# VectorE and ScalarE in source order, and 0.6 of a weight unit per round, in an attention-and-FFN kernel

## The chip, the cores and the metric

The kernel runs on one core of one Trainium2 chip. The metric is the device time of one execution in microseconds (us). Three runs of the kernel before gave 956.33 us as the median (955.23 to 957.48).

## What is computed

Three stages follow each other; the reference, cut to what matters here:

```python
q_s, k_s = q * scale, k * scale                      # 4 batches, 8 heads, 576 tokens, 64 wide
h = einsum('bhsd,md->bhsm', x, omega) - sum(x*x)/2   # phi, 128 features
q_p, k_p = exp(h - max(h)) / sqrt(m)
num = q_p @ (k_p.T @ v); den = q_p @ sum(k_p)
x = num / (den + 1e-6)                               # 2304 tokens, 512 wide
xn = x / rms(x) * rms_g
x = (silu(xn @ w_gate) * (xn @ w_val)) @ w_out       # FFN, 1536 wide
logits = x @ w_gate2                                 # routes 288 tokens to each of 8 experts
out[mask_e] = relu(x[mask_e] @ w1[e]) @ w2[e]
```

The FFN weights arrive as 64-bit floats and the chip turns them into 32-bit ones. Matrix products that need the precision are done as three products of a high and a low part.

## The kernel before

**Rounds.** The first stage is a loop over 93 rounds (`run_tick`, L748). Each round starts one of 88 items: a K item (a projection of keys, features, and k-times-v sums) or a Q item (half of a tile of queries). An item goes through lags 0 to 5, one lag a round, so that up to six items are alive in a round: lag 0 projects (TensorE, L377 to L379, into `pp`), takes the maximum (VectorE, `mx`, L386) and exponentials (ScalarE, `ft`, L389); lag 1 multiplies K features with v (L423) or transposes Q features (L465), which ScalarE copies (`qp`, L482); lag 2 of a Q item is L469 with `dn` and `x` on VectorE (L489 to L491); lag 3 squares on ScalarE (L497); lag 4 scales `xn` on VectorE (L502); lag 5 transposes `xn` (L474), and ScalarE and VectorE write its high and low parts `xh` (L512) and `xl` (L513). At the end of a round the input of the next item is split: a K item's `kh` on ScalarE and `kl` on GpSimd (L352, L353), a Q item's `qh` on VectorE and `ql` on GpSimd (L372, L373). The next round's projection needs both.

**FFN steps.** From round 25 on a round also runs an FFN half-step ("step" below): 12 matmuls (L605 to L607) of one 512-token block j against one 128-wide slice f of the gate (v = 0) or value (v = 1) weights, into one of the two `gv` buffers in PSUM. After a gate step ScalarE takes tanh (L616) and VectorE multiplies (`th`, L617); after a value step VectorE multiplies (`hp` L625 for block 0, `th` L629 for the others). There are 120 steps. Blocks share two buffers, so before a third block is begun the loop at L756 runs the remaining steps of the oldest block at once. Steps that don't fit into the rounds follow behind them.

**Units.** A unit converts 512 columns of weights: a load of 512 KB from HBM (L529, three buffers `ws`), lag 0 a magnitude on ScalarE (L533, into one of three buffers `dw`), lag 1 three shift-and-or operations on VectorE (L537 to L539, called words below), lag 2 a ScalarE cast (L561) and a GpSimd subtraction (L562) into the weight tile `wc`. Behind lag 1 of a unit the load three units ahead is issued. 24 units (two for each f) make the gate and value weights. 12 more make the output weights; these also use TensorE (L576, L580) and hold a `gv` buffer from lag 2 to lag 3. A step runs only if both units of its f are converted; a step with outstanding logits (L643) also needs the output unit of that slice.

**What sets the order.** TensorE works in the order of the source (`manual_schedule`, L778). The other engines' orders come from a scheduler that ranks instructions by priority when the program is built; the attention work has a priority 200 places ahead of its source position. On the chip each engine takes its instructions in the order built, and waits at the first that isn't ready.

**The pace.** `conv_pe` (L731) adds a pace to an account and starts a unit for each whole one: 0.5 a round up to round 24, 1.0 from round 25 while gate and value units are left, then 0.5. From round 25, while such units are left, L771 to L776 do a second helping in each round: one more unit and one more step. So six rounds (25 to 30) run two units and two steps each.

Of the kernel before, what the change touches and what calls it, by code (L numbers as in the profile page):

```python
# [31 lines left out]
KF = FF // 128  # L32
# [11 lines left out]
EARLY = 6  # L44
LOADS = 9
SKIP = 2
SUB = 1
PACE = (0.5, 1.0, 0.5)
FFN_AT = 25
AHEAD_A = 200  # L50
HB = 6
# [239 lines left out]
def kernel(ctx, tc, qT, kT, v1, om, wgv, rms, wo, wg2, w1, w2, cfd, trd, cid, out, dbg=None):  # L291
# [307 lines left out]
    def ffn_pe(j, f, v):  # L599
        n = WIDTH[j]  # L600
        pg = psG.tile([128, BLK], F32, name="gv")
        w = wsl[f].rearrange("p l (v k m) -> p l v k m", k=KD, v=2)
        xh, xl = xblk[j]
        for k in range(KD):
            nc.tensor.matmul(pg[:, :n], w[:, 0, v, k], xh[:, k, :n], start=(k == 0), stop=False)  # L605
            nc.tensor.matmul(pg[:, :n], w[:, 0, v, k], xl[:, k, :n], start=False, stop=False)  # L606
            nc.tensor.matmul(pg[:, :n], w[:, 1, v, k], xh[:, k, :n], start=False, stop=(k == KD - 1))  # L607
        return pg[:, :n]

    def ffn_el(j, f, v, pg):  # L610
        n = WIDTH[j]
        nh = n // HB2
        if v == 0:
            fst["th"] = fp.tile([128, BLK], F32, name="th")
            th = fst["th"][:, :n]
            nc.scalar.activation(th, pg, AF.Tanh, scale=0.5)  # L616
            nc.vector.scalar_tensor_tensor(th, th, 1.0, pg, op0=OP.add, op1=OP.mult)  # L617
            return
        th = fst["th"][:, :n]
        hp = fp.tile([128, BLK // HB2, 2, HB2], F32R, name="hp")  # L620
        hf = hp.bitcast(F32)
        dst = h_dr[nh * j:nh * j + nh] if nh > 1 else h_dr[NT // HB2 - 1:]
        dst = dst[:, :, f].rearrange("b p x -> p b x")
        if j == 0:
            nc.vector.scalar_tensor_tensor(hf[:, :, 0], pg.rearrange("p (b t) -> p b t", b=nh), 0.5,  # L625
                                           th.rearrange("p (b t) -> p b t", b=nh), op0=OP.mult, op1=OP.mult)
            nc.sync.dma_start(dst[:, :, :HB2], hf[:, :, 0])
            return
        nc.vector.scalar_tensor_tensor(th, pg, 0.5, th, op0=OP.mult, op1=OP.mult)  # L629
        h = th.rearrange("p (b t) -> p b t", b=nh)  # L630
        nc.scalar.copy(hp[:, :nh, 0], h)  # L631
        nc.gpsimd.tensor_sub(hp[:, :nh, 1], h, hp[:, :nh, 0])  # L632
        nc.sync.dma_start(dst, hf[:, :nh].rearrange("p b l t -> p b (l t)"))
        fq.append((j, f, hp))

    def ffn_lg(j, f, hp):
        n = WIDTH[j]
        nh = n // HB2
        if f == 0:
            st["lg", j] = (psL if j else psB).tile([2 * E, BLK], F32, name="lg" if j else "late", bufs=1)  # L640
        wv = wog[:, f].rearrange("p a e -> p (a e)")
        lg = st["lg", j][:, :n].rearrange("p (b t) -> p b t", b=nh)
        nc.tensor.matmul(lg, wv, hp[:, :nh, 0], start=(f == 0), stop=False)  # L643
        nc.tensor.matmul(lg, wv, hp[:, :nh, 1], start=False, stop=(f == KF - 1))
        if f == KF - 1:
            ls = fp.tile([2 * E, BLK], F32, name="th")
            nc.scalar.copy(ls[:, :n], st.pop(("lg", j))[:, :n])
            lgs.append((j, ls))

    def ffn_rank():  # L650
        for j, ls in lgs:
            n, c = WIDTH[j] // 128, j * BLK // 128
            pl = psL.tile([128, BLK // 128, 2 * E], F32, name="lg")
            for i in range(n):
                nc.tensor.transpose(pl[:, i, :], ls[:, i * 128:(i + 1) * 128], ident[:2 * E, :2 * E])
            lt = fp.tile([128, BLK // 128, E], F32, name="lt")
            nc.scalar.copy(lt[:, :n], pl[:, :n, E:])
            nc.vector.tensor_add(L[:, c:c + n, :], pl[:, :n, :E], lt[:, :n])
            rks.extend(range(c, c + n, 2))
        lgs.clear()  # L660

    def ffn_rank_el():
        for c0 in rks:
            ranks(nc, fp, cf[:, C_T:C_N].rearrange("p (a b) -> p a b", b=E), L, R, c0, 2)
        rks.clear()

    def ffn_step_pe():
        if not ready or ready[0][1:] not in gvs or (fq and fq[0][1] not in wogs):
            return False
        j, f, v = ready.pop(0)  # L670
        pg = ffn_pe(j, f, v)
        if (f, v) == (KF - 1, 1):
            del xblk[j]
        ffn_rank()
        if v and fq:
            ffn_lg(*fq.pop(0))
        fst["el"] = (j, f, v, pg)
        return True

    def ffn_step_el():  # L680
        if "el" in fst:
            j, f, v, pg = fst.pop("el")
            ffn_el(j, f, v, pg)
            ffn_rank_el()
            return j, f, v
        return None


    items = []
# [3 lines left out]
    useq = [WgvUnit(f, g) for f in range(KF) for g in range(2)] + [WoUnit(f) for f in range(KF)]  # L693
# [30 lines left out]
    def warm(n):  # L724
        for _ in range(n):
            nc.tensor.matmul(sink, idle[:, :128], idle[:, 128:], start=True, stop=True)

    NLAG = 6
    conv = dict(live=[], due=0.0, next=0, load=3)

    def conv_pe(pace):  # L731
        conv["due"] += pace
        conv["live"] = [(lag + 1, u) for lag, u in conv["live"] if lag < 3]
        while conv["due"] >= 1 and conv["next"] < len(useq):
            conv["due"] -= 1
            conv["live"].append((0, useq[conv["next"]]))
            conv["next"] += 1
        for lag, u in conv["live"]:
            u.pe(lag)

    def conv_el():
        for lag, u in conv["live"]:
            u.el(lag)
            if lag == 1 and conv["load"] < len(useq):
                useq[conv["load"]].load()
                conv["load"] += 1

    def run_tick(tick):  # L748
        live = [(lag, items[tick - lag]) for lag in range(NLAG) if 0 <= tick - lag < len(items)]
        conv_pe(PACE[0] if tick < FFN_AT else PACE[1] if conv["next"] < 2 * KF else PACE[2])  # L750
        with tc.high_priority(offset=AHEAD_A):
            for lag, it in live:
                it.pe(lag)
        ffn_step_pe()
        for lag, it in live:
            if lag == 5 and isinstance(it, QItem) and it.hf and it.g0 // BLK not in xblk:  # L756
                while len(xblk) > 1:
                    ffn_step_el()
                    if not ffn_step_pe():
                        conv_el()  # L760
                        conv_pe(1)
        with tc.high_priority(offset=AHEAD_A):
            for lag, it in live:
                it.el(lag)
            if tick + 1 < len(items):
                items[tick + 1].split()
        conv_el()
        if tick + AHEAD < len(items):
            items[tick + AHEAD].load()
        ffn_step_el()  # L770
        if tick >= FFN_AT and conv["next"] < 2 * KF:  # L771
            for r in range(SUB):
                conv_pe(1)
                ffn_step_pe()
                conv_el()
                ffn_step_el()  # L776

    with tc.manual_schedule(engines={mybir.EngineType.PE}):  # L778
        warm(10)
        for tick in range(len(items) + NLAG - 1):  # L780
            run_tick(tick)
            if tick < 2:
                warm(4)
    ac.close()


# [342 lines left out]
```

## Time and profile before

| | us |
|---|---|
| profiled execution | 960.06 |
| its span, first to last instruction | 958.3 |
| TensorE busy | 931.0 (97%) |
| VectorE busy | 525.4 (55%) |
| ScalarE busy | 388.4 (41%) |
| GpSimd busy | 230.4 (24%) |

The mean granted clock of TensorE is 0.992. The profile's chain of waits is 69% TensorE and 19% issue. A busy time is an average over the attention stage (up to about 395 us, with FFN steps in it from 62 us on), the rest of the FFN, the routing and the experts; TensorE is the busiest in each, so an idle stretch of TensorE is what a change can gain or lose.

### The profile page before, as it was taken

What the parts mean: (1) busy time and instruction counts of PE and PEld (TensorE: products, weight loads), DVE (VectorE), ACT (ScalarE), POOL (GpSimd) and SP (SyncE); (2) the same over time, 40 slices, a digit from 0 to 9 for tenths busy, and PEclk for the clock granted to TensorE, in tenths of its full rate; (3) what the DMA queues carried; (4) which work ended last, traced back from release to release, by engine and by line L of the source; (5) the groups of instructions that cost most, each with busy time, mean ns of one, the idle gap of its engine ahead of it and who ended that gap; (6) DMA issues with size and microseconds to landing.
All of it is one profiled execution on the core that took longest, in us unless ns stands there. A gap on an engine that the chain in (4) does not pass through costs nothing.

```text
span 958.3 us, 16626 instructions
## 1 busy us (share of the span) xinstructions
PE 931.0 (97%) x6419; PEld 809.7 (84%) x6419; DVE 525.4 (55%) x1199; ACT 388.4 (41%) x897; POOL 230.4 (24%) x287
## 2 busy tenths in 40 slices
PE   9998899999999999999999999999998999999996
PEld 7786689988888888877789777777788999999996
DVE  4899946742453335432244466666653565566652
ACT  6975445754554445522233110001003544444441
POOL 1365411322323313444334100000013221212111
PEclk9999999999999999999999999999999999999998
DMA  8547654452222221645665476766632666666550
GB/s 288 177 151 214 209 175 126 142 198 86 88 81 89 75 77 56 212 148 178 220 200 191 134 208 198 219 193 196 188 100 65 199 194 189 197 186 203 160 177 26
DMA packets 117151, 153.67 MB, mean 160 GB/s; under 512 B 6224, under 2 KB 78544, under 8 KB 117072
## 3 DMA queue, kind: packets, MB, share of 16 engines
q1 hardware_dynamic: 111264, 138.32, 46.6%
q0 software_dynamic: 3072, 9.44, 3.1%
q10 hardware_dynamic: 2736, 4.85, 1.3%
q8 instruction: 50, 0.82, 0.4%
q14 instruction: 29, 0.24, 0.1%
HBM read 108.55 MB, written 44.04 MB: 159 GB/s over the span
## 4 chain that ended last, share of the span: by engine, by line
PE 69%; issue 19%; DVE 6%; POOL 4%; ACT 1%; DMA 1%; POOLq 0%; ACTq 0%; SPq 0%; DVEq 0%
PE py L905 16%; PE gv L605 9%; PE gv L607 9%; PE gv L606 9%; PE pm L469 3%; PE pm L423 3%; POOL out_dram L1038 2%; PE cnt L177 2%; PE pm L465 2%; DVE dw L538 2%; PE pp L382 1%; PE pp L377 1%; PE pp L379 1%; POOL xh L954 1%; PE pp L378 1%
## 5 line engine op out<-in xcount | busy, mean ns | idle before, releaser
L605 PE MATMUL gv<-xh,wc 128*128 128x512 f32 (+1 forms) x480 | 184.6, 385 | 9.1 <-DVE th L617 7.9
L606 PE MATMUL gv<-xl,wc 128*128 128x512 f32 (+1 forms) x480 | 178.3, 372 | 1.5 <-DVE xl L513 1.5
L607 PE MATMUL gv<-xh,wc 128*128 128x512 f32 (+1 forms) x480 | 179.1, 373 | 0.0
L905 PE MATMUL py<-wc,ht 128*128 128x512 f32 x648 | 167.3, 404 | 0.0
L905 PEld LDWEIGHTS py<-wc,ht 128*128 128x128 f32 x648 | 114.9, 189 | 19.1
L605 PEld LDWEIGHTS gv<-xh,wc 128*128 128x128 f32 x480 | 91.5, 191 | 26.6 <-DVE th L617 8.5
L606 PEld LDWEIGHTS gv<-xl,wc 128*128 128x128 f32 x480 | 91.6, 191 | 16.2 <-DVE xl L513 2.2
L607 PEld LDWEIGHTS gv<-xh,wc 128*128 128x128 f32 x480 | 91.0, 190 | 16.4
L389 ACT ACTIVATE ft<-pp,mx 128x128 f32<-128x128 f32 x320 | 92.1, 372 | 19.6 <-DVE mx L386 17.8
L617 DVE SCALAR_TENSOR_TENSOR th<-th,gv 128x512 f32<-128x512 f32 (+1 forms) x60 | 37.8, 631 | 93.9 <-ACT th L616 93.9
L632 POOL TENSOR_TENSOR hp<-th,hp 128x512 fp32r<-128x512 f32 (+1 forms) x48 | 57.1, 1189 | 131.5 <-ACT hp L631 113.5
L876 DVE TENSOR_TENSOR wc<-ws,wc 128x512 fp32r<-128x512 f32 x128 | 84.8, 683 | 0.0
L1016 PE MATMUL ph<-exh,wc 128*128 128x288 f32 x256 | 78.1, 305 | 2.3 <-DVE ehl L1020 2.3
L1026 PE MATMUL py<-ehh,wc 128*128 128x288 f32 x256 | 77.7, 304 | 0.0
L1018 PE MATMUL ph<-exh,wc 128*128 128x288 f32 x256 | 76.8, 300 | 0.0
L1017 PE MATMUL ph<-exl,wc 128*128 128x288 f32 x256 | 76.6, 299 | 0.0
L1027 PE MATMUL py<-ehl,wc 128*128 128x288 f32 x256 | 76.0, 297 | 0.0
L1028 PE MATMUL py<-ehh,wc 128*128 128x288 f32 x256 | 75.9, 296 | 0.0
L916 ACT COPY ys<-py 128x512 f32<-128x512 f32 x18 | 10.6, 587 | 147.8 <-PE py L905 147.3
L886 ACT CAST wc<-ws 128x1024 fp32r<-128x1024 f32 x64 | 67.0, 1047 | 2.4 <-ACT ys L916 2.4
L386 DVE TENSOR_REDUCE mx<-pp 128x4 f32<-128x512 f32 (+1 forms) x88 | 56.0, 637 | 18.1 <-PE pp L379 9.3
L616 ACT ACTIVATE th<-gv 128x512 f32<-128x512 f32 (+1 forms) x60 | 33.2, 553 | 69.7 <-PE gv L607 64.4
(200 smaller groups left out, 1745.7 us busy)
## 6 DMA issues: line engine op xcount, KB each, us to landing
ws<-in_w_dram SPq DMA_DIRECT2D x64, 512.0 KB, 3.6
ht<-h_dr SPq DMA_DIRECT2D x54, 512.0 KB, 4.1
h_dr<-hp SPq DMA_DIRECT2D x36, 512.0 KB, 2.8
ws<-in_wgv_dram SPq DMA_DIRECT2D x24, 512.0 KB, 4.2
h_dr<-hp SPq DMA_DIRECT2D x24, 256.0 KB, 3.4
ws<-in_wo_dram SPq DMA_DIRECT2D x12, 512.0 KB, 3.6
h_dr<-ht SPq DMA_DIRECT2D x12, 512.0 KB, 3.0
y_dr<-ys ACTq DMA_DIRECT2D x18, 256.0 KB, 4.2
```

Source lines behind the costliest of these rows:

```text
L389: nc.scalar.activation(ft[:n, g], pp[:n, g], AF.Exp, bias=mx[:n, g:g + 1])
L605: nc.tensor.matmul(pg[:, :n], w[:, 0, v, k], xh[:, k, :n], start=(k == 0), stop=False)
L606: nc.tensor.matmul(pg[:, :n], w[:, 0, v, k], xl[:, k, :n], start=False, stop=False)
L607: nc.tensor.matmul(pg[:, :n], w[:, 1, v, k], xh[:, k, :n], start=False, stop=(k == KD - 1))
L876: nc.vector.tensor_sub(w[:, 1, h], sv[:, h], w[:, 0, h])
L905: nc.tensor.matmul(py, ht[:, i4, a], w[:, l, f % 2], start=(f == 0 and n == 0), stop=(f == KF - 1 and n == 2))
L1016: nc.tensor.matmul(ph, w[:, 0, k, m], xh[:, k], start=(k == 0), stop=False)
L1017: nc.tensor.matmul(ph, w[:, 0, k, m], xl[:, k], start=False, stop=False)
L1018: nc.tensor.matmul(ph, w[:, 1, k, m], xh[:, k], start=False, stop=(k == KD - 1))
L1026: nc.tensor.matmul(py, w[:, 0, k], hh[:, k], start=(k == 0), stop=False)
L1027: nc.tensor.matmul(py, w[:, 0, k], hl[:, k], start=False, stop=False)
L1028: nc.tensor.matmul(py, w[:, 1, k], hh[:, k], start=False, stop=(k == KE - 1))
```

## The change

While gate and value units are left, the rounds are recorded under a manual schedule of TensorE, VectorE and ScalarE: these three keep the order of the source. The second helping in a round is gone, and the pace is 0.6 in place of 1.0. The stretch goes from round 25 until the last gate/value unit is no longer the newest one, which is round 45. Before and after it only TensorE is in source order, as before. In the lists below the changed kernel's line numbers are one lower than before.

```diff
-SUB = 1
-PACE = (0.5, 1.0, 0.5)
+PACE = (0.5, 0.6, 0.5)
...
         ffn_step_el()
-        if tick >= FFN_AT and conv["next"] < 2 * KF:
-            for r in range(SUB):
-                conv_pe(1)
-                ffn_step_pe()
-                conv_el()
-                ffn_step_el()
 
     with tc.manual_schedule(engines={mybir.EngineType.PE}):
         warm(10)
-        for tick in range(len(items) + NLAG - 1):
+        for tick in range(FFN_AT):
             run_tick(tick)
             if tick < 2:
                 warm(4)
+    with tc.manual_schedule(engines={mybir.EngineType.PE, mybir.EngineType.DVE, mybir.EngineType.Activation}):
+        tick = FFN_AT
+        while conv["next"] < 2 * KF or conv["live"][-1][1] is useq[2 * KF - 1]:
+            run_tick(tick)
+            tick += 1
+    with tc.manual_schedule(engines={mybir.EngineType.PE}):
+        for tick in range(tick, len(items) + NLAG - 1):
+            run_tick(tick)
```

**First place: ScalarE at round 25**, from the magnitude of unit 11 (`dw_788`) to what feeds round 27. `th_868` and `th_871` are the tanh of the first FFN step, `kh_935` and `kh_915` the split keys that round 27 projects, `ft_926` and `ft_906` the exponentials of round 26. Before:

```order
L533 ACTIVATE dw_788<-ws_579 128x512
L561 CAST wc_608<-dw_611 128x512
L616 ACTIVATE th_868<-gv_833 128x512
L561 CAST wc_785<-dw_694 128x512
L561 CAST wc_785<-dw_788 128x512
L352 CAST kh_1003<-kt_864 128x256
L533 ACTIVATE dw_862<-ws_659 128x512
L389 ACTIVATE ft_926<-pp_894,mx_924 128x128 x4
```

Now:

```order
L532 ACTIVATE dw_788<-ws_579 128x512
L560 CAST wc_608<-dw_611 128x512
L560 CAST wc_785<-dw_694 128x512
L560 CAST wc_785<-dw_788 128x512
L532 ACTIVATE dw_865<-ws_659 128x512
L615 ACTIVATE th_871<-gv_836 128x512
L388 ACTIVATE ft_906<-pp_874,mx_904 128x128 x4
L511 CAST xh_911<-pm_886 128x4x64
L351 CAST kh_915<-kt_748 128x128
```

The tanh now stands behind the casts of units 10 and 11 and behind the magnitude of unit 12, which reads the load `ws_659`; the split keys for round 27, which stood ahead of the exponentials of round 25 (three places above the first list), now stand behind those of round 26.

**Second place: VectorE in rounds 40 and 41.** `hp_1600` belongs to the value step of round 40, `mx_1633` to the projection of round 41, `qh_1647` to the split of the queries that round 42 projects. Before, the words in such a round and the cast of the next queries stand like this (`hp_1678` is the product of a value step, `mx_1716` the maximum of the projection behind it):

```order
L537 TENSOR_SCALAR dw_1867<-dw_1867 128x512
L490 RECIPROCAL dn_1661<-dn_1661 128x4
L538 SCALAR_TENSOR_TENSOR dw_1867<-ws_1552,dw_1867 128x512
L491 TENSOR_TENSOR x_1660<-pm_1633,dn_1661 128x256
L539 SCALAR_TENSOR_TENSOR dw_1867<-ws_1552,dw_1867 128x512
L625 SCALAR_TENSOR_TENSOR hp_1678<-gv_1638,th_1614 128x2x256
L372 CAST qh_1862<-qt_1737 128x512
L386 TENSOR_REDUCE mx_1716<-pp_1686 128x4
```

Now:

```order
L512 TENSOR_TENSOR xl_912<-pm_1554,xh_911 128x4x64
L536 TENSOR_SCALAR dw_1530<-dw_1530 128x512
L537 SCALAR_TENSOR_TENSOR dw_1530<-ws_1303,dw_1530 128x512
L538 SCALAR_TENSOR_TENSOR dw_1530<-ws_1303,dw_1530 128x512
L624 SCALAR_TENSOR_TENSOR hp_1600<-gv_1559,th_1534 128x2x256
L385 TENSOR_REDUCE mx_1633<-pp_1603 128x4
L488 TENSOR_SCALAR dn_1642<-pm_1615 128x4
L489 RECIPROCAL dn_1642<-dn_1642 128x4
L490 TENSOR_TENSOR x_1581<-pm_1615,dn_1642 128x256
L501 SCALAR_TENSOR_TENSOR xn_1586<-x_1462,ss_1587,gr_71 128x512
L371 CAST qh_1647<-qt_1532 128x512
```

The words stand behind `xl`, and the cast of the queries is the last of its round instead of the first.

**Third place: VectorE in rounds 68 to 70**, behind the steps that the loop at L756 runs at once (`xl_3305` and `xl_3304` are lag 5 of round 68). Before:

```order
L617 SCALAR_TENSOR_TENSOR th_3276<-th_3276,gv_3263 128x512
L629 SCALAR_TENSOR_TENSOR th_3276<-gv_3279,th_3276 128x512
L513 TENSOR_TENSOR xl_3305<-pm_3238,xh_3304 128x4x128
L386 TENSOR_REDUCE mx_3339<-pp_3317 128x4
L617 SCALAR_TENSOR_TENSOR th_3357<-th_3357,gv_3326 128x512
L386 TENSOR_REDUCE mx_3394<-pp_3360 128x4
```

Now:

```order
L616 SCALAR_TENSOR_TENSOR th_3228<-th_3228,gv_3215 128x512
L628 SCALAR_TENSOR_TENSOR th_3228<-gv_3231,th_3228 128x512
L616 SCALAR_TENSOR_TENSOR th_3275<-th_3275,gv_3262 128x512
L628 SCALAR_TENSOR_TENSOR th_3275<-gv_3278,th_3275 128x512
L512 TENSOR_TENSOR xl_3304<-pm_3190,xh_3303 128x4x128
L385 TENSOR_REDUCE mx_3330<-pp_3321 128x4
L591 CAST wog_74<-gv_3257 128x8
L592 TENSOR_TENSOR wog_74<-gv_3257,wog_74 128x8
L385 TENSOR_REDUCE mx_3380<-pp_3350 128x4
```

Four steps instead of two are run at once, the last output unit (`gv_3257`) is among them, and between the maxima of rounds 69 and 70 there is no FFN step.

## Rows read from the trace of the kernel before

**Rows 1.** windows: length, busy us of PE, PEld, DVE, ACT, POOL, PEclk, DMA share, GB/s

```profile
75.00:100.00 25.00, 20.62 (x100) 17.34 (x99) 24.69 (x33) 13.22 (x28) 13.77 (x10) 0.93 0.70 217
100.00:125.00 25.00, 20.49 (x99) 16.77 (x98) 20.37 (x29) 12.43 (x31) 9.13 (x9) 0.93 0.73 228
275.00:300.00 25.00, 25.00 (x158) 21.74 (x157) 12.74 (x29) 12.94 (x36) 7.95 (x12) 1.00 0.25 86
```

**Rows 2.** what TensorE waited for, 55 to 200 us: total us, times, longest

```profile
PE gv L605 <- DVE th L617: 7.9, 4, 2.4
PE gv L606 <- DVE xl L513: 1.5, 2, 0.8
PE gv L605 <- DVE hp L625: 1.0, 1, 1.0
```

**Rows 3.** VectorE's words by line, 55 to 132 us: busy us, mean ns

```profile
L538 DVE SCALAR_TENSOR_TENSOR dw<-ws,dw 128x512 int32<-128x512 int32 x19 | 17.8, 947 | 0.3
L539 DVE SCALAR_TENSOR_TENSOR dw<-ws,dw 128x512 int32<-128x512 int32 x19 | 16.4, 872 | 0.3
L537 DVE TENSOR_SCALAR dw<-dw 128x512 int32<-128x512 int32 x20 | 13.8, 694 | 1.6 <-ACT dw L533 1.6
```

**Rows 4.** windows of 4 us with a lowered TensorE clock

```profile
88.00:92.00 4.00, 3.29 (x9) 2.62 (x10) 3.97 (x7) 1.72 (x5) 2.10 (x2) 0.65 0.73 219
...
116.00:120.00 4.00, 3.97 (x10) 3.12 (x11) 3.90 (x8) 2.18 (x7) 0.46 (x1) 0.57 0.91 269
```

**Rows 5.** VectorE in order of time, 50 to 82 us

```profile
65.78 1.28 DVE L539 SCALAR_TENSOR_TENSOR dw<-ws,dw 128x512 int32<-128x512 int32 x2
...
69.36 0.68 DVE L617 SCALAR_TENSOR_TENSOR th<-th,gv 128x512 f32<-128x512 f32 x1
```

**Rows 6.** the SP queue in order of time, 59 to 80 us

```profile
60.85 0.33 SPq L529 DMA_DIRECT2D ws<-in_wgv_dram  x1
...
66.48 5.03 SPq L529 DMA_DIRECT2D ws<-in_wgv_dram  x3
```

**Rows 7.** ScalarE in order of time, 50 to 82 us

```profile
62.70 1.14 ACT L389 ACTIVATE ft<-pp,mx 128x128 f32<-128x128 f32 x4
65.00 0.68 ACT L533 ACTIVATE dw<-ws 128x512 f32<-128x512 f32 x1 [1.16 <-DMA ws<-in_wgv_dram]
66.49 0.62 ACT L561 CAST wc<-dw 128x512 fp32r<-128x512 f32 x1 [0.81 <-DVE dw L539]
67.02 0.59 ACT L616 ACTIVATE th<-gv 128x512 f32<-128x512 f32 x1
```

**Rows 8.** TensorE in order of time, 60 to 110 us: start, length

```profile
63.26 0.50 PE L606 MATMUL gv<-xl,wc 128*128 128x512 f32 x1 [0.85 <-DVE xl L513]
...
65.67 0.39 PE L607 MATMUL gv<-xh,wc 128*128 128x512 f32 x1
```

**Rows 9.** TensorE in order of time, 134 to 165 us

```profile
144.50 0.36 PE L377 MATMUL pp<-omh,qh 128*128 128x256 f32 x1
...
146.53 0.48 PE L605 MATMUL gv<-xh,wc 128*128 128x512 f32 x1
...
149.37 0.95 PE L580 MATMUL gv<-wg2s,dw 128*128 128x8 f32 x8
```

**Rows 10.** GpSimd in order of time, 50 to 82 us

```profile
62.82 1.28 POOL L562 TENSOR_TENSOR wc<-dw,wc 128x512 fp32r<-128x512 f32 x1
```

**Rows 11.** VectorE in order of time, 134 to 165 us: start, length

```profile
141.60 0.42 DVE L537 TENSOR_SCALAR dw<-dw 128x512 int32<-128x512 int32 x1
...
142.05 0.69 DVE L538 SCALAR_TENSOR_TENSOR dw<-ws,dw 128x512 int32<-128x512 int32 x1
...
142.99 0.68 DVE L539 SCALAR_TENSOR_TENSOR dw<-ws,dw 128x512 int32<-128x512 int32 x1
...
145.36 0.43 DVE L372 CAST qh<-qt 128x512 fp32r<-128x512 f32 x1 [0.33 <-PE pp L378]
...
149.30 0.75 DVE L502 SCALAR_TENSOR_TENSOR xn<-x,ss,gr 128x512 f32<-128x512 f32 x1 [1.70 <-POOL ss L499]
```

## The prediction

> **What bounds the kernel now.** I read the profile in this order: the windows by stretch, to see where TensorE is idle; its waits there; the same stretch on VectorE; then the engines in order of time around the points that the change moves. TensorE is busy all 25 us of a later window, but only 20.6 and 20.5 us in the two from 75 us on, where its clock is also 0.93 instead of 1.00 and VectorE is busy 24.7 and 20.4 us [rows 1]. These are the rounds with two units and two steps. TensorE waits there for `th` (7.9 us in 4 waits), for `hp` (1.0 us), and for `xl` (1.5 us in two waits, one before and one behind these rounds) [rows 2]. So VectorE bounds these rounds: its words are 17.8 + 16.4 + 13.8 = 48 us of work [rows 3], and the products that release `gv` stand among them. From 55 to 200 us nearly all of TensorE's idle time is in these rows. What the change can give is there; its price must lie in new waits of TensorE.
>
> **What goes.** A round now has one step and 0.6 of a unit: about 0.6 x 1.8 us of words where there were 2 x 1.8 or more. The waits for `th` and `hp` in rounds 25 to 30 end: 7.9 + 1.0. Of the waits for `xl` I count 1.3 of 1.5 as gone: two words move behind the first `xl`. [...] Sum: **13.3 us less**. TensorE's work is the same; the number of steps that are left behind the rounds (46) is the same too, counted from the code with either pace: what rounds 25 to 30 no longer do is done in round 68 and 90 in one go.
>
> **What comes: the first queue.** Source order puts the tanh of the first step behind the magnitude of unit 12 (first place). That reads a load whose buffer is set free by the last word of unit 9. In the trace this word ends at 65.78 + 0.64 [rows 5] and the load is issued at 66.48 [rows 6]; the load before took from 60.85 [rows 6] until ScalarE was released at 65.00 [rows 7], 4.1 us. So the data is there at 70.6; magnitude 0.68 and tanh 0.59 [rows 7], `th` 0.68 [rows 5] and a maximum of the same length, four exponentials 1.14 [rows 7], two short copies (`xh`, `kh`, a half and a quarter as wide as the 0.62 us cast [rows 7], taken as 0.7 together), and 0.5 for `kl` and handing over: 70.6 + 5.0 = 75.6 us before round 27 can project. TensorE is there sooner: its first step ends at 65.67 + 0.39 [rows 8], less 0.65 as `xl` comes sooner, 65.4; round 26 takes 2.03 of attention and 2.84 for its step, as in the round at 144.50 [rows 9]: 70.3. Gap 5.3 us. In the rows `th` and the keys are hoisted ahead of this magnitude, so nothing of it is paid today. If GpSimd's 1.28 us subtractions [rows 10] fall on the words, as seen in their means of 947 and 872 ns against 0.69 and 0.68 undisturbed [rows 3, 11], the load goes out 1.3 later: 6.6. If the load were no obstacle, the word of unit 11 (0.42 + 0.69 + 0.68 = 1.8 us [rows 11], from 66.4) and its cast would still hold the tanh: some 3. I take **6.0** (3.0 to 7.2). Rounds 28 and 29 catch up, since `hp` and the maximum again stand behind a word and the keys behind the exponentials: **1.5** (0 to 2.5).
>
> [...]
>
> **The query rounds.** In round 40 the order on ScalarE is tanh, exponentials, copy, square, `xh`, and on VectorE `xl` waits for that, with the words and `hp` behind it (second place). Then round 41's maximum, `dn` to `x`, `xn`, `qh`, and on GpSimd `ql`, must end before round 42's third matmul. From the end of round 39's step: 0.59 + 0.68 + 0.68 + 1.14 for tanh, `th`, maximum and exponentials, 1.24 for two passes as wide as the cast, 0.8 for half-wide `xh` and `xl`, 1.79 for words, 0.68 + 0.68 for `hp` and maximum, 0.8 for `dn` to `x` (an estimate, between mx and xn), 0.75 + 0.43 for `xn` and `qh` [rows 11], 1.28 for `ql` as the other 512-wide subtraction [rows 10]: 11.5, with handing over 11.8. TensorE's two rounds are 2 x 4.87 [rows 9] plus about 0.45 of an `xn` transpose: 10.2. It waits 1.6. Rounds 44 and 45 have the same chain with keys at its end; 1.2 each as an estimate. In all **4.0** (1.0 to 6.0; in round 33 to 38 no link is late). In the rows `qh` stands ahead of the maximum, out of this chain.
>
> **Leaving the stretch.** At round 46 the words of the last value unit and the first output unit stand in front of `th` and of the transposes of that output unit: two more words are 3.6 us of VectorE against one round of slack. **1.3** (0 to 3).
>
> **Round 68.** Four steps are run at once with the last output unit among them (third place). It holds one of the two `gv` buffers, so the last value step waits for tanh and `th` of its gate step: 0.59 + 0.68 + 0.2 = 1.5. Round 69 has no step to cover its maximum and exponentials (0.68 + 1.14 and handing over, less the projection that TensorE has): 1.1. Together **2.6** (1.5 to 3).
>
> **The clock.** Slow stretches followed runs of waits of about 2 us each; a single gap of 6 us is longer than any here. I count one slow window, **1.7** (0 to 3.4) [rows 4].
>
> [...]
>
> **The sum.** 6.0 + 1.5 + 4.0 + 1.3 + 2.6 + 1.7 = 17.1 comes, 13.3 goes: 3.8 slower. The bounds are 3.0 + 0 + 1.0 + 0 + 1.5 + 0 = 5.5 and 7.2 + 2.5 + 6.0 + 3.0 + 3.0 + 3.4 = 25.1, so 7.8 faster to 11.8 slower. The profiled execution of 960.06 lies 3.7 above the median of 956.33; on the median's scale the forecast is **960.1 us**, the bounds 948.5 and 968.1.
>
> **Rivals.** *Faster:* VectorE's burst is the only thing that ever delays TensorE, and the new queues have slack. It decides by the load of unit 12: if it lands within 2.5 us of its issue, the first gap is 3.0; then rounds 28 and 29 cost 0.5, the queries 1.0, leaving 0, round 68 2.6, the clock 0: 7.1 against 13.3, 6.2 faster, 950.1 us. For it: TensorE is busy throughout query rounds from 275 to 300 us [rows 1], and loads are fewer per round than before. Against: 4.1 us in the rows, and VectorE's 24.7 of 25 us just ahead. *No change:* the gap comes, but the queries and the leaving cost 1.0 in all, since the projection's first two products need only `qh`: 6.0 + 1.5 + 1.0 + 2.6 + 1.7 = 12.8, 0.5 faster, 955.8 us. *Slower by more:* the clock falls twice and the queries cost 6.0: 3.8 + 1.7 + 2.0, 963.8 us. *The change doesn't hold:* VectorE's list has casts of queries of round 55 and later inside the stretch, so source order binds only the stretch's own instructions; such a cast waiting for its load would block words and products alike. I count that within the queries' upper bound.
>
> **Chances.** A measurement of this kernel can tell about 0.2% (1.9 us) from no change. The forecast with the slower rival has 0.50, no change 0.22, the faster rival 0.28: the gap at round 27 is the surest part, the size of the rest is not. The range takes in the faster rival and most of the upper bound: 947.5 to 965.5 us. The forecast's own case is 958.5 to 965.5.
>
> **What would show it.** In the profile after: no waits of TensorE for `th` near 76 to 116 us; one gap of 5 to 7 us in front of L377 or L379 near 70 us, with ScalarE waiting for a `ws` load ahead of its first tanh; waits of L379 for `ql` or `kl` of 1 to 2 us between about 130 and 165 us; at round 68, near 270 us, a wait for `th` of 1.5 us and one for `ft` of 1. The forecast is wrong if the gap at 70 us is under 3 us, or if the waits between 120 and 300 us sum to under 3 us.

## The result, and the profile after

The changed kernel takes **962.25 us** as the median of 4 runs (960.57 to 964.34), the kernel before 956.09 beside it (955.23 to 957.48): ratio **1.0064**, 95% interval 1.0049 to 1.0079. The forecast was 960.1. It is slower, as predicted, by 6.2 us where 3.8 were forecast.

| us | before | after |
|---|---|---|
| profiled execution | 960.06 | 960.57 |
| its span | 958.3 | 958.8 |
| TensorE busy | 931.0 | 929.8 |
| VectorE / ScalarE / GpSimd busy | 525.4 / 388.4 / 230.4 | 523.9 / 387.3 / 229.9 |
| TensorE idle, 50 to 200 | 11.5 | 12.5 |
| first routing matmul | 718.0 | 720.8 |

The two profiled spans differ by 0.5 us only. The profiled execution of the changed kernel is the fastest of its four, 1.7 below their median, while that of before lies 3.7 above its own, with a disturbance in the routing, where both kernels do the same. Its window there, and that of the changed kernel (columns: length, busy us of PE, PEld, DVE, ACT, POOL, PEclk, DMA share, GB/s):

```profile
725.00:750.00 25.00, 22.72 (x163) 22.48 (x162) 9.26 (x19) 8.33 (x17) 4.14 (x5) 0.93 0.36 110
```

```profile
725.00:750.00 25.00, 23.49 (x178) 23.10 (x177) 10.27 (x21) 9.17 (x18) 5.54 (x6) 1.00 0.35 111
```

TensorE idle 2.3 us (a wait for `ehl`, the low part of an expert's hidden values) and a clock of 0.93 (25 x 0.07 = 1.75 us) make 4.0 us before, 1.5 us now. The wait for `ehl` goes with the occasion and not with the kernel: it is in none of the profiles of the first four experiments, and in every profile of the eight later ones, whatever their order (2.2 to 2.3 us). So the comparison is better made at the first routing matmul, 2.8 us later in the changed kernel's profile, and 5.0 later (723.0) in that of its repeat below.

**Where the time went.** What TensorE waits for from 55 to 200 us in the changed kernel (total us, times, longest), against [rows 2]:

```profile
PE pp L376 <- ACT kh L351: 8.0, 3, 7.0
PE pp L378 <- POOL kl L352: 1.7, 3, 1.0
PE gv L575 <- DVE dw L538: 0.9, 1, 0.9
PE pp L378 <- POOL ql L372: 0.8, 2, 0.5
```

The waits for `th` and `hp`, 8.9 us, are gone, and that for `xl` went from 1.5 to 0.4. In their place stand 7.0 us in one piece for the keys of round 27, and 3.5 us of small waits for `kh`, `kl` and `ql`. The windows that answer to [rows 1]:

```profile
50.00:75.00 25.00, 17.73 (x123) 15.40 (x121) 20.66 (x36) 16.82 (x46) 11.62 (x14) 0.92 0.45 143
75.00:100.00 25.00, 23.90 (x120) 20.48 (x121) 13.53 (x23) 11.98 (x36) 7.36 (x9) 0.88 0.48 148
100.00:125.00 25.00, 25.00 (x150) 21.99 (x149) 17.28 (x30) 13.86 (x38) 9.14 (x8) 1.00 0.56 165
```

VectorE falls from 24.7 to 13.5 and from 20.4 to 17.3 us, TensorE gains 3.3 and 4.5 us of busy time there, and pays 5.3 in the window ahead of them (23.05 busy before, 17.7 now), with a lowered clock (0.92 and 0.88) in two windows. The gap on TensorE (start, length, what, and in brackets the idle time ahead of it and what ended it):

```profile
68.44 0.39 PE L606 MATMUL gv<-xh,wc 128*128 128x512 f32 x1
75.80 0.58 PE L376 MATMUL pp<-omh,kh 128*128 128x256 f32 x1 [6.97 <-ACT kh L351]
```

ScalarE and VectorE in it, which answer to [rows 5, 7]:

```profile
66.81 1.22 ACT L560 CAST wc<-dw 128x512 fp32r<-128x512 f32 x2 [1.40 <-DVE dw L538]
71.12 0.62 ACT L560 CAST wc<-dw 128x512 fp32r<-128x512 f32 x1 [3.08 <-DVE dw L538]
71.64 0.66 ACT L532 ACTIVATE dw<-ws 128x512 f32<-128x512 f32 x1
72.21 0.58 ACT L615 ACTIVATE th<-gv 128x512 f32<-128x512 f32 x1
74.14 1.14 ACT L388 ACTIVATE ft<-pp,mx 128x128 f32<-128x128 f32 x4 [1.35 <-DVE mx L385]
...
75.41 0.34 ACT L351 CAST kh<-kt 128x128 fp32r<-128x128 f32 x1
```

```profile
67.31 0.42 DVE L536 TENSOR_SCALAR dw<-dw 128x512 int32<-128x512 int32 x1
67.76 1.66 DVE L537 SCALAR_TENSOR_TENSOR dw<-ws,dw 128x512 int32<-128x512 int32 x1
69.45 1.63 DVE L538 SCALAR_TENSOR_TENSOR dw<-ws,dw 128x512 int32<-128x512 int32 x1
72.82 0.69 DVE L616 SCALAR_TENSOR_TENSOR th<-th,gv 128x512 f32<-128x512 f32 x1 [1.73 <-ACT th L615]
```

GpSimd and the SP queue, which answer to [rows 6, 10]:

```profile
67.51 3.03 POOL L561 TENSOR_TENSOR wc<-dw,wc 128x512 fp32r<-128x512 f32 x2 [2.82 <-ACT wc L560]
```

```profile
66.84 4.63 SPq L528 DMA_DIRECT2D ws<-in_wgv_dram  x3
```

Read from the end: `kh` stands behind the exponentials and `xh`, these behind the maximum and `th`, that behind the tanh, that behind the magnitude of unit 12 and the cast of unit 11. This cast was released at 71.1 by VectorE's last word of unit 11 (69.45 + 1.63). The words of that unit took 0.42 + 1.66 + 1.63 us, beside two GpSimd subtractions of 3.03 us together. The magnitude shows no wait for its load, the first of three issued from 66.84 on; ScalarE reached it at 71.64. TensorE was done with the tanh's step at 64.07 (its last matmul, L606, at 63.67 + 0.40); ScalarE took the tanh at 72.21 and was idle for 1.40 and 3.08 us in between, each time in front of a cast that stands ahead of it.

Round 68 is late as forecast, but near 304 us:

```profile
PE gv L604 <- DVE th L616: 1.5, 1, 1.5
```

### The profile page after: what moved, and what is told of

Its sections match the earlier page's. It is cut to its first block, busy times and chain, and to the rows that moved or that the text cites. A ratio compares the mean times of both kernels' runs of the same rounds, so it can differ in the third digit from the quotient of the medians.

```text
span 958.8 us, 16616 instructions
## 1 busy us (share of the span) xinstructions
PE 929.8 (97%) x6419; PEld 807.2 (84%) x6419; DVE 523.9 (55%) x1199; ACT 387.3 (40%) x897; POOL 229.9 (24%) x287
## 4 chain that ended last, share of the span: by engine, by line
PE 58%; issue 18%; POOL 4%; DVE 1%; ACT 0%; POOLq 0%; ACTq 0%
PE py L906 16%; PE gv L604 8%; PE gv L606 8%; PE gv L605 8%; POOL out_dram L1039 2%; PE cnt L176 2%; PE pm L468 2%; PE pm L422 2%; POOL xh L955 1%; PE pp L376 1%; PE lg L643 1%; PE gv L579 1%; PE lg L642 1%; PE pp L378 1%; PE pp L377 1%
## 5 line engine op out<-in xcount | busy, mean ns | idle before, releaser
L606 PE MATMUL gv<-xh,wc 128*128 128x512 f32 (+1 forms) x480 | 178.2, 371 | 0.0
L606 PEld LDWEIGHTS gv<-xh,wc 128*128 128x128 f32 x480 | 90.6, 189 | 16.3
L1018 PE MATMUL ph<-exl,wc 128*128 128x288 f32 x256 | 75.8, 296 | 0.0
```

Source lines behind the costliest of these rows:

```text
L1018: nc.tensor.matmul(ph, w[:, 0, k, m], xl[:, k], start=False, stop=False)
```

## The experiments

Ratios are against the kernel before on the same chip and the same occasion; its median was 954.5 us beside the first four runs and 958.3 to 958.7 beside the others, so times of different occasions are not compared as they stand. The theory of the prediction (A in the texts below): ScalarE's queue in source order opens the gap at round 27 and delays keys and queries later; the slower pace by itself gives back the waits of rounds 25 to 30. Its rival (B): the slower pace costs, since steps and output units come later, and the order is neutral.

| run | ratio (95%) |
|---|---|
| the change, repeated | 1.0062 (1.0049 to 1.0075) |
| pace only | 0.9975 (0.9966 to 0.9984) |
| order only | 1.0029 (1.0019 to 1.0038) |
| stretch four rounds later | 1.0022 (1.0014 to 1.0031) |
| split first | 0.9990 (0.9980 to 1.0000) |
| step first | 1.0119 (1.0101 to 1.0136) |
| no subtraction, units 8 to 11 | 1.0028 (1.0013 to 1.0042) |
| pace only, output units 0.75 | 0.9993 (0.9982 to 1.0003) |
| split first, pace 0.7 | 1.0055 (1.0033 to 1.0076) |
| split first, output units 0.55 | 1.0012 (0.9999 to 1.0025) |
| **VectorE alone in source order** | **0.9965 (0.9951 to 0.9978)** |
| ScalarE alone in source order | 1.0058 (1.0037 to 1.0078) |

### The change, repeated

> The changed kernel once more, unaltered, because its profiled span lies only 0.5 us above the one of before while its median lies 6.2 us above. Theory A (source order puts the tanh of the first step and the keys of round 27 behind unit 12's magnitude, which waits for its load): 960 to 964 us again, ratio 1.005 to 1.008, and again one gap of about 7 us near 76 us. If the profiled span is the better witness: about 956.6 us, ratio 1.0005.

960.74 us against 954.53. The gap of 6.9 us is there again and so are the 6.2 us, so the nearly equal spans were the chance of two executions: one with the disturbance, one the fastest of four.

### Pace only, order only

```diff
 pace only
-    with tc.manual_schedule(engines={PE, DVE, Activation}):
+    with tc.manual_schedule(engines={PE}):
 order only (in run_tick, and PACE = (0.5, 1.0, 0.5))
+        if tick >= FFN_AT and conv["next"] < 2 * KF:
+            for r in range(SUB): conv_pe(1); ffn_step_pe(); conv_el(); ffn_step_el()
```

> Only the pace of the change (0.6 of a unit and one step per round); VectorE and ScalarE stay in the scheduler's order. Theory A (source order is what costs; the slower pace by itself ends the waits for th of 75 to 116 us): no gap near 76 us, th waits under 2 us up to 120 us, 946 to 950 us, 0.990 to 0.993 of before. Theory B (the slower pace itself costs, since the steps that are put off come back in round 68 and the output units come later, and the order is neutral): 960 to 964 us as with the whole change.

> Only the order of the change: VectorE and ScalarE in source order from round 25 on, with two units and two steps per round as before. Theory A: the waits for th of before stay or grow (7.9 us) and the gap before round 27 comes on top, 962 to 975 us, 1.006 to 1.02. Theory B (order neutral, pace costs): 955 to 957 us, 1.000.

The pace alone gives 2.4 us, not 6 to 10; the order alone costs 2.7, less than thought; together they cost 6.2, so they don't add, and neither A nor B has it right. Waits of TensorE with the pace alone, 55 to 200 us, and VectorE's first word (the shift), 55 to 132 us (count, busy us, mean ns):

```profile
PE pm L422 <- ACT ft L388: 1.9, 2, 1.7
PE gv L605 <- DVE xl L512: 1.6, 1, 1.6
PE pm L464 <- ACT ft L388: 1.2, 2, 0.9
```

```profile
L536 DVE TENSOR_SCALAR dw<-dw 128x512 int32<-128x512 int32 x19 | 13.6, 715 | 1.7 <-ACT dw L532 1.6
```

19 units' words stand in that stretch, about as many as before [rows 3]: the scheduler draws words and magnitudes forward, whatever the pace says. The waits for `th` end all the same; that this is because one step per round leaves TensorE attention work to do is argued, not shown. The longest wait for `ft` stands behind the words (one runs from 94.75 until the maximum starts at 95.85); the one for `xl` stands behind an `xn` that waited 0.7 us for GpSimd's `ss`. With the changed kernel's order VectorE runs the words of only 11 units there:

```profile
L536 DVE TENSOR_SCALAR dw<-dw 128x512 int32<-128x512 int32 x11 | 6.4, 589 | 0.0
```

The order alone has the same queue on ScalarE, but TensorE does not wait for the keys of round 27 at all (the line numbers of this run are those of before):

```profile
74.51 0.50 PE L605 MATMUL gv<-xh,wc 128*128 128x512 f32 x1 [1.38 <-DVE th L617]
80.13 0.28 PE L377 MATMUL pp<-omh,kh 128*128 128x256 f32 x1
118.68 0.39 PE L377 MATMUL pp<-omh,kh 128*128 128x256 f32 x1 [2.46 <-ACT kh L352]
```

```profile
78.74 0.34 ACT L352 CAST kh<-kt 128x128 fp32r<-128x128 f32 x1
```

There ScalarE is done with `kh` for round 27 at 79.1 us, later than the 75.8 of the changed kernel, but TensorE reaches that projection only at 80.1: the two steps of round 26, from 74.5 on, kept it at work, and the queue costs the 1.4 us in front of them. A wait for `kh` (2.5) comes at 118.7, behind the first round that has one step again. The helping that the change takes out was the cover of the gap.

### Which engine's order

```diff
-    with tc.manual_schedule(engines={PE, DVE, Activation}):
+    with tc.manual_schedule(engines={PE, DVE}):          (VectorE alone)
+    with tc.manual_schedule(engines={PE, Activation}):   (ScalarE alone)
```

> The changed kernel with VectorE alone in source order in the stretch; ScalarE is left to the scheduler, which puts the key casts and the tanh of the first step ahead of the casts of units 10 and 11 again. If ScalarE's order makes the gap (prediction): the gap of 7.0 shrinks to 2 to 3, left by the exponentials behind the magnitude of unit 12, the waits for kl and kh near 160 us end, those for ql (0.8) stay; 4 to 7 us below the changed kernel, ratio to before 0.999 to 1.002. If VectorE's words in source order are what holds the round: a gap of 5 or more stays, 1.004 to 1.007.

> The changed kernel with ScalarE alone in source order in the stretch; VectorE is left to the scheduler. If ScalarE's order makes the gap (prediction): 5 to 8 us in front of round 27 as in the changed kernel, and waits for kl and kh near 160 us; since VectorE's words are drawn forward again, waits for th on top; ratio to before 1.003 to 1.010. If VectorE's order makes the gap: under 3 us there, and 0.997 to 1.000 as with the pace alone.

This decides it. With ScalarE left to the scheduler the change has the lowest ratio of all versions, 954.27 against 958.67; with ScalarE in source order and VectorE free it is as slow as the whole change, 963.28. These two ran beside each other: 9.0 us lie between them, and 6.9 at the first routing matmul of their profiles (713.2 and 720.1). By the ratios ScalarE's order costs 7.9 us without VectorE's (0.0083 of 956) and 9.3 with it (0.0097), each give or take about 2; VectorE's makes no difference that the intervals show. TensorE's waits from 55 to 200 us with VectorE alone, and ScalarE there:

```profile
PE pm L422 <- ACT ft L388: 2.7, 2, 2.6
PE pp L378 <- POOL ql L372: 2.0, 3, 1.0
```

```profile
67.02 0.59 ACT L615 ACTIVATE th<-gv 128x512 f32<-128x512 f32 x1
67.50 0.40 ACT L351 CAST kh<-kt 128x256 fp32r<-128x256 f32 x1
...
70.61 1.22 ACT L560 CAST wc<-dw 128x512 fp32r<-128x512 f32 x2 [2.44 <-DVE dw L538]
71.74 0.66 ACT L532 ACTIVATE dw<-ws 128x512 f32<-128x512 f32 x1
72.42 1.14 ACT L388 ACTIVATE ft<-pp,mx 128x128 f32<-128x128 f32 x4
```

Tanh and keys stand ahead of the casts of units 10 and 11 again; 2.6 us are left, for exponentials behind them, and `ql` waits 2.0 us in three places, more than the 0.8 expected. VectorE runs the words of 12 units from 55 to 132 us, about as in the changed kernel. ScalarE alone in source order gives 11 or 12 too; there VectorE sits idle 7.6 us for the magnitudes (L532), which are ScalarE's work:

```profile
L536 DVE TENSOR_SCALAR dw<-dw 128x512 int32<-128x512 int32 x11 | 8.8, 802 | 7.6 <-ACT dw L532 7.6
```

The expectation for ScalarE alone was wrong in one place: the gap in front of round 27 is 2.1 us, not 5 to 8. So ScalarE's order makes the loss, but a single gap of 7 us only together with VectorE's.

```profile
PE pp L376 <- ACT kh L351: 3.7, 2, 2.1
PE pp L378 <- POOL kl L352: 2.0, 3, 1.4
PE gv L605 <- DVE xl L512: 1.6, 1, 1.6
```

```profile
70.87 0.62 ACT L560 CAST wc<-dw 128x512 fp32r<-128x512 f32 x1 [1.95 <-DVE dw L538]
...
73.69 0.34 ACT L351 CAST kh<-kt 128x128 fp32r<-128x128 f32 x1
```

The chain on ScalarE is the one of the changed kernel, with `kh` at 73.7 in place of 75.4: the scheduler runs VectorE's maximum ahead of `th`, so that the exponentials don't wait 1.35 us for it. TensorE came to it 3 us later, held up by `xh` (0.8) and `xl` (1.6); its time is lost in more, shorter waits and in windows at a lowered clock (0.93 from 50 to 75, 75 to 100 and 150 to 175 us). Each order has its own small waits: those for `ql` are there with VectorE alone and not with ScalarE alone, those for `kh` and `kl` the other way round.

### What the gap is made of

```diff
 no subtraction (WgvUnit, lag 2)
-                nc.gpsimd.tensor_sub(w[:, 1, s_], self.t, w[:, 0, s_])
+                if 8 <= 2 * f + self.g <= 11:
+                    nc.scalar.copy(w[:, 1, s_], self.t)
+                else: nc.gpsimd.tensor_sub(w[:, 1, s_], self.t, w[:, 0, s_])
 four rounds later
-        for tick in range(FFN_AT):
+        for tick in range(FFN_AT + 4):
```

> The changed kernel with the low parts of units 8 to 11 written by a ScalarE copy; GpSimd's subtraction of these four units is left out, so their low part is not the difference. In the trace of the changed kernel the nine words of units 9 to 11 take 8.5 us on VectorE from 62.6 us on, three of them beside two subtractions of 1.5 us. Theory G (a GpSimd subtraction stretches the words beside it): the words go back to 0.42, 0.69 and 0.68 us, 5.4 us for the nine, and the gap in front of round 27 falls from 7.0 to 3.5 to 5. Theory L (prediction: the load of unit 12 holds the magnitude ahead of the tanh): ScalarE then waits for the load itself and the gap is 5 to 6.5. If the words are stretched by something else: 7.0 again. Time 1 to 4 us below the changed kernel.

The words of unit 11 are back at 0.41 + 0.69 + 0.69 us, and ScalarE then waits for the load of unit 12 itself:

```profile
66.55 0.41 DVE L536 TENSOR_SCALAR dw<-dw 128x512 int32<-128x512 int32 x1
66.99 0.69 DVE L537 SCALAR_TENSOR_TENSOR dw<-ws,dw 128x512 int32<-128x512 int32 x1
67.72 0.69 DVE L538 SCALAR_TENSOR_TENSOR dw<-ws,dw 128x512 int32<-128x512 int32 x1
```

```profile
70.05 0.66 ACT L532 ACTIVATE dw<-ws 128x512 f32<-128x512 f32 x1 [0.47 <-DMA ws<-in_wgv_dram]
```

The gap is 5.05 us. Both G and L hold: the load, issued at 66.08 here, is there at 70.05, 4.0 us later. In the changed kernel, issued at 66.84, it would be there near 70.8, and the stretched words and the cast behind them let ScalarE come to the magnitude at 71.64. The two chains end 0.8 us apart, so to mend the words alone, which also sends the load off 0.8 sooner, takes 2 of the 7 us. Whether a fourth load buffer would take the rest wasn't tried.

> The change with its source-order stretch begun four rounds later (round 29): rounds 25 to 28 keep the pace of 0.6 and one step, in the scheduler's order. Theory A: the gap of 7 us in front of round 27's projection and the slow clock behind it go, unless a magnitude that waits for a load stands ahead of a tanh at round 29 too (then a gap of up to 3 us there); 952 to 957 us, 5 to 10 below the changed kernel. Theory B: 960 to 964 us.

956.53 us: four rounds of scheduler's order at the start take back 3.8 of the 6.2 us. In place of the gap of 7 stands a wait of 2.4 us for `ft`, so that much of A holds.

### Where in the round the split and the step stand

```diff
 split first (in the stretch)
+                items[tick + 1].split()
             for lag, it in live:
                 it.el(lag)
-                items[tick + 1].split()
 step first (in the stretch)
+        ffn_step_el()
         conv_el()
...
-        ffn_step_el()
```

> The changed kernel with the split of the next item's keys or queries recorded ahead of the round's other work on VectorE and ScalarE, in the source-order stretch alone. If the place of the split at the end of a round is what costs (prediction): the waits for kh, kl and ql behind 85 us (3.2 us in the changed kernel) end, and the gap in front of round 27 shrinks from 7.0 to 4.5 to 5.5, since the key cast no longer stands behind the exponentials and xh; 4 to 6 us below the changed kernel, ratio to before 0.999 to 1.002. If VectorE's words hold everything: as the changed kernel, 1.005 to 1.007.

> The changed kernel with the tanh and products of a round's FFN step recorded ahead of the weight conversion of the round, in the source-order stretch alone. If the tanh behind the magnitude is what opens the gap (prediction): the gap of 7.0 shrinks by the tanh and th, 1.3, to 5.7; the words move behind hp, so the wait for dw in front of the output unit's transposes grows by about 1; in all 0 to 2 us below the changed kernel. If the casts of units 10 and 11, which wait for VectorE's words, hold ScalarE whatever stands behind them: the gap stays at 5.5 to 7.

Split first, 55 to 200 us:

```profile
PE gv L575 <- DVE dw L538: 2.8, 1, 2.8
PE pp L376 <- ACT kh L351: 2.4, 1, 2.4
```

No wait for `ql` is left, and `kh` waits 2.4 us in place of 8.0, all of it in front of round 27, where 4.5 to 5.5 were expected; 0.0072 of 956 = 6.9 us come back, more than expected. The wait for `dw` in front of the first output unit's transposes grew from 0.9 to 2.8, which wasn't expected. In the trace VectorE takes `xn` (0.7 late for GpSimd's `ss`), `xl`, `th` and `hp` between the first word of that unit, at 163.24, and the end of its last, at 168.7.

Step first was a miss. The gap shrank to 5.1 as it should, but the whole lost 5.4 us more (0.0057 of 956):

```profile
PE pp L376 <- ACT kh L351: 7.3, 4, 5.1
PE pp L378 <- POOL ql L372: 2.7, 3, 0.9
```

The words now stand between `hp` and the next round's maximum, so that chain, which ends in keys and queries, holds three words, 1.8 us, more. That reading rests on the order in the source; no run takes it apart.

### Attempts at the small waits

```diff
-PACE = (0.5, 0.6, 0.5)
+PACE = (0.5, 0.6, 0.75)   (with pace only)
+PACE = (0.5, 0.7, 0.5)    (with split first)
+PACE = (0.5, 0.6, 0.55)   (with split first)
```

> The pace of the change alone (scheduler's order) with 0.75 of an output unit per round behind the gate and value units in place of 0.5, so that the last output unit is done before round 68. If the output unit among the steps run at once in round 68 is what makes the last of them wait (prediction): the wait for th of 1.5 us near 304 us ends, and the time falls by 1.5 against the pace alone (952.4), to 950 to 951.5. Against: the words of the output units crowd VectorE sooner, and waits of about 1 us come back between 175 and 250 us: 952 to 953.

> The changed kernel with the split first in a round of the stretch, and 0.7 of a unit per round in place of 0.6. The stretch then ends three rounds sooner and the last output unit two rounds before round 68. If the waits left with the split first (dw 2.8 at the end of the stretch, th 1.5 near 304 us) come from where the last value unit and the output units fall, both go: 949 to 953 us where before is 954.5, ratio 0.993 to 0.997. If 0.7 of a unit per round is already too much for VectorE, waits for th or kl come back between 80 and 150 us: 0.998 to 1.002.

> The changed kernel with the split first in a round of the stretch, and 0.55 of an output unit per round in place of 0.5. The stretch is as it was; the last output unit starts two rounds sooner (round 65). The wait for th of 1.5 us near 304 us ends; the wait for dw of 2.8 at the end of the stretch stays, if it comes from the last value unit and the first output unit standing next to each other. 1.5 us below the split first alone: ratio 0.996 to 0.999. The gv buffers held by two output units that follow each other closely can give back 0.6 for each such pair.

None gained. With 0.75 the wait of 1.5 us in round 68 ended as expected, and four others took its place, 3.6 us from 170 to 310 us:

```profile
PE gv L575 <- DVE wog L592: 1.9, 3, 0.6
PE gv L575 <- DVE th L616: 1.7, 1, 1.7
```

All four are waits of an output unit's transposes for a `gv` buffer, three times held by the output unit ahead, once by a step: output units closer together hold these buffers against each other. With 0.55 the wait near 304 us ended too, but a wait of 0.6 of the same kind came up, and one of 1.4 for `th` near 242 us. With 0.7 the wait for `dw` stayed (3.1 us), and behind it and a `kl` wait the mean clock from 150 to 175 us fell to 0.66. Ending the stretch three rounds sooner didn't remove the wait for `dw`; why that unit's words stand so late stays open.

## Why the prediction was right, and where it wasn't

| term | predicted | measured |
|---|---|---|
| `th`, `hp` go | -8.9 | -8.9 |
| `xl` goes | -1.3 | -1.1 |
| slow windows of 75 to 125 go | -3.1 | -3.5 (PEclk of two windows) |
| first queue, round 27 | 6.0 | 7.0, repeat 6.9 |
| rounds 28, 29 | 1.5 | 0.3 |
| query rounds and the keys behind | 4.0 | 3.2 |
| leaving the stretch | 1.3 | 0.9 |
| round 68 | 2.6 | 1.5 |
| clock behind the gap | 1.7 | 2.5 (2.0 from 76 to 80 us, 0.5 to 84) |

The 3.1 us for the slow windows are a term of the forecast's 13.3 that no run shows by itself; what the runs showed in its place is the 3.5 (2 x 25 x 0.07, from the clocks in [rows 1]) and, in the changed kernel, a clock of 1.00 in the two windows of [rows 4], 88 to 92 and 116 to 120 us.

The sum of the right column is 1.9 slower against 3.8 forecast and 6.2 by the medians; the profile's own figure at the first routing matmul is 2.8, and the repeat's is 5.0, with a further slow stretch there near 185 us. So the terms account for this pair of executions to about 1 us; where the other executions of the changed kernel, up to 964.3, lose the rest isn't shown. The range, 947.5 to 965.5 us, took in the faster rival and no change as well, so that the time lies in it says little; what tells the cases apart is the gap (against the faster rival) and the 4.1 us of the queries and the leaving (against no change, which had 1.0). Right were the side, the place, the mechanism and the order of sizes: one gap ahead of L376 near 70 us behind ScalarE's queue, small waits after it, the `th` wait of round 68. The faster rival's condition, a load that lands within 2.5 us of its issue, wasn't met: 4.0 in the run without the subtractions, and 4.3 as the median of these loads in the changed kernel's profile. The slower rival's time, 963.8, is nearer than the forecast, but neither its second fall of the clock nor its 6.0 for the queries came.

What failed, step by step:

- **The cause of the 6.0.** The prediction took the load as the last link ("ScalarE waiting for a ws load ahead of its first tanh") and the words as a second-best ("some 3"), with undisturbed durations of 1.8 us. They took 3.7 beside the subtractions, and with the cast behind them they set when the magnitude began. The end of the queue came out (75.6 forecast, 75.8 measured) because two errors cancel: the magnitude began at 71.6 in place of 70.6, and the chain from it to the projection took 4.2 us, not 5.0. This was luck as much as reading. That the gap is 7.0 and not 5.3 lies at its other end: TensorE was through with round 26 at 68.8, not 70.3.
- **"A round now has one step and 0.6 of a unit".** The words were credited to the pace. The pace alone leaves 19 units in the stretch; it takes hold only with ScalarE or VectorE in source order. And with only VectorE in source order the gain comes without most of the price. The prediction never asked which of the two engines' order carried which term: the waits for keys come with ScalarE's, those for `ql` with VectorE's.
- **The cover.** The second helping was costed as load on VectorE alone. Its step also was TensorE's work during ScalarE's queue: order alone waits 1.4 us there, for `th`, where the changed kernel waits 7.0 for `kh`.
- **Query rounds.** The chain of 11.8 us was too long by 1: waits of 0.3 and 0.5 for `ql` in place of 1.6. The two rounds with keys at the chain's end came out as forecast, 1.2 each (0.17 for `kh` and 1.03 for `kl` near 157 us, 0.83 and 0.34 near 165).
- **Round 68.** The 1.1 for `ft` didn't come, and the place was 304 us, not 270.

Unit 11's two words with two inputs took 1.66 and 1.63 us beside two subtractions of 3.03 us together in the changed kernel, and 0.69 each in the run without the subtractions. How a subtraction holds a word up isn't shown.

## What to carry to other kernels

Source order is not one switch: set it for each engine by itself, and ask of each what stands last in the source but is needed first. On ScalarE here that was the tanh and the key split, behind casts that wait for another engine. Before a helping is taken out of a round because it loads one engine, look at which queue its matmuls cover.

A version that beats both kernels came out of this: pace 0.6, one step, and source order for VectorE but not for ScalarE, 0.9965 of before (954.27 against 958.67 us). The pace alone (0.9975) can't be told from it by the intervals, so that source order for VectorE gains anything over the pace alone isn't shown.

## What the runs showed of the hardware

A gap of 2.6 us in front of a matmul left the granted clock at 1.00 with VectorE alone; one of 2.45 us, with 0.4 and 0.3 behind it, was followed by 0.66 with the split first; the gap of 7.0 went with 0.50 for two windows, of which only the second has TensorE at work. The windows (columns as above), of VectorE alone, split first and the changed kernel:

```profile
72.00:76.00 4.00, 3.16 (x17) 2.80 (x18) 3.93 (x6) 2.51 (x7) 2.58 (x3) 1.00 0.66 246
```

```profile
72.00:76.00 4.00, 3.51 (x13) 3.02 (x14) 2.46 (x5) 1.71 (x6) 1.17 (x2) 0.66 0.52 175
```

```profile
72.00:76.00 4.00, 0.20 (x1) 0.21 (x2) 1.71 (x4) 2.39 (x8) 1.26 (x2) 0.50 0.47 133
76.00:80.00 4.00, 4.00 (x15) 3.68 (x16) 2.88 (x6) 1.02 (x4) 0.28 (x1) 0.50 0.44 116
```

So the clock was lower behind the gap of 7.0 us, and behind the 6.9 of the repeat (0.50 from 76 to 80 us); behind gaps of about 2.5 us it went either way (1.00 and 0.66), so a short gap here can't be priced by its length alone.

The prediction had not counted on one more thing: not only the words with two inputs but also the shift (L536), which has one, took longer beside a subtraction here. Two of them took 2.42 us from 62.56 on in the changed kernel, with a subtraction from 63.22 to 64.69, and 1.32 from 62.89 on in the run without subtractions. The first took 0.98 and 0.99, beside the split of keys on GpSimd in both runs, the second 1.51 and 0.41.
